# Local attention and two feed-forward layers on one core: loads under way limited to four

## The chip, the cores and the metric

The kernel runs on one core of a Trainium2 chip. A core has a matrix engine (PE, with its weight loads PEld), a vector engine (DVE), a scalar engine (ACT), a general engine (POOL) and a sync engine (SP), each with its own program, and 16 DMA engines that move data between the chip's memory and the on-chip buffers. The metric is the device time of one execution in microseconds, as the median of several runs. Before the change it is 648.09 us (three runs, 647.77 to 649.55).

## What is computed

Three stages follow one another on 1536 tokens (2 batches of 768), all in float32:

```python
# attention: 8 heads of 64, window 16, blocks of 32
k_sum = k.reshape(B, H, nb, block, D).max(axis=3)
v_sum = v.reshape(B, H, nb, block, D).mean(axis=3)
scores_l = scale * q @ k.T            # kept where |i - j| < 16
scores_s = scale * q @ k_sum.T + log(block)
a = softmax(concat(scores_l, scores_s)); x = a @ concat(v, v_sum)
# layer 1: RMS norm, gate and value (512 -> 1536), back to 512
xn = x / rms * rms_g
y = (silu(xn @ w_gate) * (xn @ w_val)) @ w_out
# layer 2: 512 -> 2048 -> 512
r = maximum(y @ w_in, 0); out = (s * r * r + b) @ w_out2
```

## The kernel before

**Attention, then the layers.** The attention works on 12 tiles of 128 tokens (two halves of 64 queries, four head pairs). For a tile PE multiplies queries with a key window and with the block maxima (line 522), DVE adds the mask and finds the extremes (541), ACT takes the exponentials (548), PE transposes the weights (559) and multiplies with the value window and the block means (578), DVE normalises (596), and after the RMS norm (611 to 619) PE transposes the tile into `x` (627). From about 70 us on the matrix products of the layers take over (`mm12`, lines 726 to 730, and 849 to 852). Each weight comes as a 512 KB tile of 64-bit words, which ACT and DVE turn into a float32 (205, 214 to 216) and which is then split into a high and a low part (227, 231).

**Loads.** Every load is a DMA that SP issues: keys `load_k` (273), queries `load_q` (440), value windows `load_v` (277), transposed values `load_vt` (290), the vector of constants (157), weights `w_load` (199). `spread_v` (312) copies the block means, 24 partitions, from one value slot to others, on the chip. SP runs its program in order: an issue that has to wait holds all issues behind it. Eight semaphores serve the loads in turn, so in the kernel before the change a load waits for the landing of the eighth load in front of it, and for whatever frees its target buffer (three query tiles, three raw weight tiles, one value buffer shared by the two batches).

**What sets the order.** The attention part is written as a list of tasks with an engine, a duration, dependencies and a rank (`plan`, from line 434 on). `give_out` plays these through a small model of the engines and so fixes the order of each engine's program. The layers' part is written out in order (`moe`).

Of the kernel before, what the change touches and what calls it, by code (L numbers as in the profile page):

```python
# [11 lines left out]
I32 = mybir.dt.int32  # L12
# [6 lines left out]
NB, NH, SEQ, HD = 2, 8, 768, 64  # L19
# [16 lines left out]
NSUB = NB * SEQ // SUB  # L36
TPS = SUB // 128
HEAD = 3
LAT = 0.09
AHEAD = 4.0  # L40
IDLE = 0.6
PTENG = ("ACT",)
QB = 3
# [11 lines left out]
def kernel(ctx: ExitStack, tc: tile.TileContext, q_t, k_t, v_w, v_t, w_gate, w_val, w_out, w_in2, w_out2, vecs, out):  # L55
    nc = tc.nc
# [19 lines left out]
    def banks(*ids):  # L76

        turn = [0]

        def take():  # L80
            i = ids[turn[0] % len(ids)]
            turn[0] += 1
            return psp.tile([128, 512], F32, tag=f"b{i}", name=f"b{i}")
        return take
# [21 lines left out]
    vec = const.tile([128, DM + 2], F32, name="vec")  # L106
    gbc, sbc, bbc = vec[:, 0:DM], vec[:, DM:DM + 1], vec[:, DM + 1:DM + 2]
    junk = const.tile([128, DM], mybir.dt.bfloat16, name="junk")
    qc = [const.tile([128, NPAIR, 2, HQ], F32, name=f"q{i}") for i in range(QB)]
# [8 lines left out]
    vt0 = xyp.tile([128, 2 * KD * SUB], F32, tag="xy", name="vt")  # L118
# [4 lines left out]
    kst = [t[:, 0:NPAIR * KL].rearrange("p (j s) -> p j s", j=NPAIR) for t in kb]  # L123
# [24 lines left out]
    def consts_mask2():  # L148
# [3 lines left out]
        for i, p0, o in ((0, 0, 0), (2, 64, HQ + WIN)):  # L152
            nc.gpsimd.tensor_copy(masks[i], m)
            nc.gpsimd.memset(masks[i][p0:p0 + 64, o:o + WIN], NEG / scale)

    def load_small():
        nc.sync.dma_start(out=vec, in_=vecs)


    later = [[] for _ in range(8)]  # L160
# [22 lines left out]
    units = []  # L183
# [12 lines left out]

    def w_load(i):
        t = rawp.tile([128, 512, 2], I32, tag="raw", name="raw")
        nc.sync.dma_start(out=t.rearrange("p f c -> p (f c)"), in_=units[i].bitcast(I32))
        raw_t[i] = t  # L200

    def w_scale(i):
# [31 lines left out]
    def w_split(i):  # L234
        w_high(i)
        w_low(i)

    steps = [w_load, w_scale, w_bits, w_split]
    used = [0]
    live = [0]  # L240
# [29 lines left out]


    def load_k(b, j):
        nc.sync.dma_start(out=kst[b][:, j], in_=k_t[b, j])

    def load_v(b, s0, n):
        t = vst[b][s0 // NTL][0:KW, s0 % NTL:s0 % NTL + n]
        nc.sync.dma_start(out=t.rearrange("p s h d -> p (s h d)"), in_=v_w[b, s0 // n])

    def ones_v(b, s0, n):
        rows = KC if s0 < (4 if b == 0 else 2) else KW  # L280
# [6 lines left out]
    vs = vt0[:, NPAIR * SEQ:NPAIR * SEQ + 512]  # L287

    def load_vt(b, j):
        nc.sync.dma_start(out=vt0[:, j * SEQ:(j + 1) * SEQ], in_=v_t[b, j])  # L290

    def sum_vt(b, j):
        c0 = j * 128 + KW
# [15 lines left out]
    def spread_v(b, s0, n):  # L309
        a = vst[b][0][KW:KC, 0:2].rearrange("p (o e) h d -> p o (e h d)", o=1).broadcast_to([NS, n // 2, 2 * NH * VH])  # L310
        o = vst[b][s0 // NTL][KW:KC, s0 % NTL:s0 % NTL + n]
        nc.sync.dma_start(out=o.rearrange("p (o e) h d -> p o (e h d)", e=2), in_=a)


    tasks = []
# [3 lines left out]
    def task(eng, us, fn, deps=(), rank=0.0, take=(), give=(), bank=None, free=(), more=0.09):  # L319

        t = dict(eng=eng, us=us, fn=fn, deps=[d for d in deps if d is not None], rank=rank, take=take, give=give,
                 bank=bank, free=free, more=more, end=None)
        tasks.append(t)
        return t
# [3 lines left out]
    def give_out():  # L328
# [22 lines left out]
        while left:  # L351
            moved = False
            for e in ("SP", "PE", "ACT", "DVE", "POOL"):
                if clock[e] > now + 1e-9:
                    continue
                for z in pending[e]:
                    t = z[2]
                    if any(d["end"] is None or d["end"] + LAT > now + 1e-9 for d in t["deps"]):
                        continue
# [25 lines left out]
                    for k, o in t["give"]:  # L385
                        ends[k][o["slot"][k]] = t["end"] + LAT
                    for o in t["free"]:
                        o["freed"] = t["end"] + LAT
                        bank_free.append((o["freed"], o["b"]))
# [13 lines left out]
            nxt += [v for k in rings for v in ends[k].values() if v > now]  # L403
            nxt += [t["end"] + LAT for t in tasks if t["end"] is not None and t["end"] + LAT > now + 1e-9]
            assert nxt, [z[2]["why"] if "why" in z[2] else (e, z[0]) for e in pending for z in pending[e][:3]]
            now = min(nxt) + 1e-6
            at = clock["PE"] + IDLE
            if now > at and any(x[0] <= at for x in bank_free) and ident_at[0]["end"] is not None and ident_at[0]["end"] + LAT < at and pending["PE"]:

# [7 lines left out]
    def dve(n):  # L417
        return 0.07 + 1.042e-3 * n

    def act(n):  # L420
        return 0.13 + 0.74e-3 * n
# [7 lines left out]
    def plan(x):  # L429
# [6 lines left out]
        def lk(b, j, rank):  # L436
            K[b, j] = task("SP", mb(128 * KL * 4), lambda: load_k(b, j), rank=rank)

        def load_q(i):
            nc.sync.dma_start(out=qc[i % QB].rearrange("p j c q -> p (j c q)"), in_=q_t[i])  # L440

        def lq(i, rank, deps=()):
            Q[i] = task("SP", mb(128 * 512 * 4), lambda: load_q(i), deps, rank=rank)

        def lvt(b, j, rank):
            VL[b, j] = task("SP", mb(128 * 768 * 4), lambda: load_vt(b, j), [SV[0, j]] if b else (), rank=rank)

        def lv(b, t, rank):
            V[b, t] = task("SP", mb(96 * 16 * VH * 4), lambda: load_v(b, 2 * t, 2), rank=rank)
            O[b, t] = task("POOL", 0.12, lambda: ones_v(b, 2 * t, 2), [V[b, t]], rank=rank)  # L450
# [10 lines left out]
        for t in range(1, NTL):  # L461
            lv(0, t, t - 1.5)
        sml = task("SP", mb(128 * 514 * 4), load_small, rank=1.2)
        for j in range(NPAIR):
            lk(1, j, 4 + j)
# [64 lines left out]
        for n, (i, g) in enumerate(us):  # L530
            b, t = divmod(i, NTL)
# [30 lines left out]
            e = PTENG[n % len(PTENG)]  # L562
# [51 lines left out]
            def do_ss(i=i):  # L614
# [5 lines left out]
                out=X_of[i], in0=X_of[i], scalar=box["ss", i][:, 1:2], in1=gbc, op0=ALU.mult, op1=ALU.mult), [S, sml], n - 1)  # L620
# [20 lines left out]
            h = task("ACT", act(512), lambda f=two_x: f(0), [ET], n - 1.2)  # L641
# [5 lines left out]
        def weight(u, rank):  # L647
            l = task("SP", mb(128 * 1024 * 4), lambda: w_load(u), rank=rank - WLEAD, take=("raw",))
            s = task("ACT", act(512), lambda: w_scale(u), [l], rank, take=("wa",))
            ops = []  # L650
            prev = s
            for k in range(3):
                def bits(k=k):
                    if k == 0:
                        ops.extend(w_ops(u))
                    ops[k]()
                prev = task("DVE", (0.45, 0.72, 0.72)[k], bits, [prev], rank + 0.1 * k, give=(("raw", l),) if k == 2 else ())
            hh = task("ACT", act(512), lambda: w_high(u), [prev], rank + 0.5, take=("wh",))
            ll = task("POOL", 1.34, lambda: w_low(u), [hh], rank + 0.5, take=("wl",), give=(("wa", s),))
            W[u] = (hh, ll)  # L660
        wr = WRANK
        for u in range(2 * HEAD + MORE):
            weight(u, wr[u] if u < len(wr) else wr[-1] + 3 * (u - len(wr) + 1))
# [5 lines left out]
        for s in range(NSUB):  # L669
            for j in range(HEAD):  # L670
                rk = FR[s] + j * FS
# [39 lines left out]
                a = task("ACT", act(512), lambda f=do_u: f(0), [got[0][2]], rr, take=("u",))  # L711
                b_ = task("DVE", dve(512), lambda f=do_u: f(1), [a], rr, free=(got[0][0],))
                c = task("DVE", dve(512), lambda f=do_v: f(0), [b_, got[1][2]], rr, free=(got[1][0],))
                d = task("ACT", act(512), lambda f=do_v: f(1), [c, *((*free_of[j], box.get("hi")) if s == 0 else ())], rr)
# [47 lines left out]
    def moe(x, ps_m):  # L762
# [24 lines left out]
        def s1(m):  # L787
            if m < HEAD:
                return
            w = next_w()  # L790
            us = [gate(m, w, s) for s in range(NSUB)]
            yield
            w = next_w()
            for s in range(NSUB):
                val(m, w, s, us[s])
            yield
# [72 lines left out]
    give_out()  # L869
    n = 2 * HEAD + MORE  # L870
    prog[:] = [n, n, n, n]
    used[0] = live[0] = 2 * HEAD
    for _ in moe(x, banks(*range(8))):
# [69 lines left out]
```

## Time and profile before

| | us |
|---|---|
| median of 3 runs | 648.09 |
| profiled execution | 647.01 |
| its span | 645.2 |
| PE busy | 622.8 |
| DVE busy | 378.1 |
| ACT busy | 259.8 |
| POOL busy | 141.7 |

The profile shows one execution. Its span runs from the first to the last instruction; some 1.8 us lie around it. A gap on an engine is put down to what ended it: another engine, a landing, or "issue", which means that the engine waited for nothing that the profile shows. The DMA tables tell how many bytes each queue moved in a stretch and what share of the 16 engines' time that took; a stretch can show more than 100%, since packets that start in it may end behind it. The chain of waits is followed back from the last instruction, at each step to what released it.

### The profile page before, as it was taken

The numbers are of one execution on the slowest core, as the hardware profiler recorded it, in microseconds if no ns is written. First come the engines' busy times: TensorE is split into PE (matmuls) and PEld (weight loads), VectorE is DVE, ScalarE is ACT, GpSimd is POOL, SyncE is SP. The second block draws the span as 40 slices with busy tenths as digits, with TensorE's granted clock in tenths as the row PEclk, the third lists the DMA queues.
The fourth block names the chain that finished last, engine by engine and source line by source line (L and its number), as shares of the span: only waits on it lengthen the run. The fifth ranks groups of instructions, "written<-read, shape, count | busy, mean of one in ns | idle before, by whom it ended". The sixth has DMA issues, their size and how long they took to land.

```text
span 645.2 us, 9632 instructions
## 1 busy us (share of the span) xinstructions
PE 622.8 (97%) x3816; PEld 514.3 (80%) x3816; DVE 378.1 (59%) x731; ACT 259.8 (40%) x524; POOL 141.7 (22%) x159
## 2 busy tenths in 40 slices
PE   5588999999999999999999999999999999999998
PEld 3576788888888888888888888888888888888886
DVE  5469886325851555544556767870388457845532
ACT  2576986334433333212333345542554045404400
POOL 2253856322311111111111111100221022103100
PEclk9889999999999999999999999999999999999999
DMA  9979622003440112221122212230212321210022
GB/s 294 230 264 257 193 60 74 1 1 98 131 130 28 42 63 66 86 61 53 62 65 69 64 65 67 65 100 31 56 46 67 94 62 42 66 61 0 2 98 99
DMA packets 17494, 55.04 MB, mean 85 GB/s; under 512 B 2000, under 2 KB 2256, under 8 KB 17448
## 3 DMA queue, kind: packets, MB, share of 16 engines
q1 hardware_dynamic: 17448, 54.42, 27.7%
q8 instruction: 30, 0.49, 0.3%
q14 instruction: 16, 0.13, 0.1%
HBM read 50.35 MB, written 3.15 MB: 83 GB/s over the span
## 4 chain that ended last, share of the span: by engine, by line
PE 91%; DVE 3%; issue 2%; DMA 1%; ACT 1%; SPq 0%; POOL 0%; POOLq 0%
PE b L726 22%; PE b L730 22%; PE b L727 22%; PE b L852 7%; PE b L850 7%; PE b L849 7%; PE b L559 2%; PE b L522 2%; PE b L578 2%; DMA vt<-in_v_t_dram 1%; PE b L627 1%; DVE vt L294 1%; DVE P L541 0%; DVE km L284 0%; ACT P L548 0%
## 5 line engine op out<-in xcount | busy, mean ns | idle before, releaser
L231 POOL TENSOR_TENSOR wl<-wa,wh 128x512 fp32r<-128x512 f32 x68 | 89.1, 1318 | 389.3 <-ACT wh L227 316.0
L726 PE MATMUL b<-x,wh 128*128 128x512 f32 x288 | 113.7, 395 | 0.1
L727 PE MATMUL b<-x,wl 128*128 128x512 f32 x288 | 112.2, 390 | 0.0
L227 ACT ACTIVATE wh<-wa 128x512 fp32r<-128x512 f32 x68 | 41.5, 627 | 97.2 <-PE b L852 45.5
L730 PE MATMUL b<-x,wh 128*128 128x512 f32 x288 | 77.8, 392 | 0.0
L850 PE MATMUL b<-wl,hg 128*128 128x512 f32 (+1 forms) x196 | 75.1, 385 | 0.0
L849 PE MATMUL b<-wh,hg 128*128 128x512 f32 (+1 forms) x196 | 75.1, 385 | 0.0
L726 PE MATMUL b<-y,wh 128*128 128x512 f32 x192 | 74.7, 389 | 0.0
L727 PE MATMUL b<-y,wl 128*128 128x512 f32 x192 | 74.7, 389 | 0.0
L831 DVE SCALAR_TENSOR_TENSOR b<-u,vec 128x512 f32<-128x512 f32 x48 | 50.7, 1057 | 35.6 <-ACT u L830 35.6
L726 PEld LDWEIGHTS b<-x,wh 128*128 128x128 f32 x288 | 54.1, 188 | 11.3 <-ACT x L638 0.4
L727 PEld LDWEIGHTS b<-x,wl 128*128 128x128 f32 x288 | 54.1, 188 | 10.7
L730 PEld LDWEIGHTS b<-x,wh 128*128 128x128 f32 x288 | 53.5, 188 | 11.0
L726 PE MATMUL b<-hg,wh 128*128 128x512 f32 x144 | 56.0, 389 | 0.0
L727 PE MATMUL b<-hg,wl 128*128 128x512 f32 x144 | 56.0, 389 | 0.0
L751 DVE SCALAR_TENSOR_TENSOR hg<-b,vec,hg 128x512 fp32r<-128x512 f32 x48 | 36.0, 749 | 28.1 <-ACT hg L750 28.1
L852 PE MATMUL b<-wh,hg 128*128 128x512 f32 (+1 forms) x196 | 51.5, 385 | 0.0
L730 PE MATMUL b<-y,wh 128*128 128x512 f32 x192 | 51.3, 389 | 0.0
L216 DVE SCALAR_TENSOR_TENSOR wa<-raw,wa 128x512 int32<-128x512 int32 x68 | 50.0, 735 | 2.0
L750 ACT ACTIVATE hg<-b,vec 128x512 fp32r<-128x512 f32 x48 | 33.0, 687 | 43.0 <-DVE b L831 43.0
L858 DVE TENSOR_TENSOR part<-b,part 128x512 f32<-128x512 f32 (+1 forms) x37 | 24.4, 673 | 43.5 <-PE b L852 43.5
L215 DVE SCALAR_TENSOR_TENSOR wa<-raw,wa 128x512 int32<-128x512 int32 x68 | 47.0, 691 | 2.0
(85 smaller groups left out, 947.2 us busy)
## 6 DMA issues: line engine op xcount, KB each, us to landing
raw<-in_w_out_dram SPq DMA_DIRECT2D x28, 512.0 KB, 3.5
raw<-in_w_in_dram SPq DMA_DIRECT2D x16, 512.0 KB, 4.1
raw<-in_w_gate_dram SPq DMA_DIRECT2D x12, 512.0 KB, 3.6
raw<-in_w_val_dram SPq DMA_DIRECT2D x12, 512.0 KB, 3.6
hg<-in_k_t_dram SPq DMA_DIRECT2D x8, 400.0 KB, 10.0
q<-in_q_t_dram SPq DMA_DIRECT2D x12, 256.0 KB, 7.1
vt<-in_v_t_dram SPq DMA_DIRECT2D x8, 384.0 KB, 8.3
out_dram<-part SPq DMA_DIRECT2D x11, 256.0 KB, 2.0
```

What stands on the lines that cost most here:

```text
L215: lambda: nc.vector.scalar_tensor_tensor(out=ai, in0=hi, scalar=-0x80000000, in1=ai, op0=ALU.bitwise_and, op1=ALU.bitwise_or),
L216: lambda: nc.vector.scalar_tensor_tensor(out=ai, in0=lo, scalar=29, in1=ai, op0=ALU.logical_shift_right, op1=ALU.bitwise_or),
L227: nc.scalar.activation(out=r(h), in_=a_t[i], func=AF.Copy)
L231: nc.gpsimd.tensor_tensor(out=r(lo), in0=a_t.pop(i), in1=high[i], op=ALU.subtract)
L726: nc.tensor.matmul(ps, r(hi[:, kk * 128:(kk + 1) * 128]), xh, start=kk == 0, stop=False)
L727: nc.tensor.matmul(ps, r(lo[:, kk * 128:(kk + 1) * 128]), xh, start=False, stop=False)
L730: nc.tensor.matmul(ps, r(hi[:, kk * 128:(kk + 1) * 128]), r(act(kk, 1)), start=False, stop=kk == 3)
L751: nc.vector.scalar_tensor_tensor(out=r(dst[1]), in0=ps, scalar=bias, in1=dst[0], op0=ALU.add, op1=ALU.subtract)
L831: after(0, lambda u=u, ps=ps: nc.vector.scalar_tensor_tensor(out=ps, in0=u, scalar=sbc[:, 0:1], in1=u, op0=ALU.mult, op1=ALU.mult))
L849: nc.tensor.matmul(acc, gh, r(ws[e][0][:, cs]), start=e == 0, stop=False)
L850: nc.tensor.matmul(acc, gh, r(ws[e][1][:, cs]), start=False, stop=False)
L852: nc.tensor.matmul(acc, r(ge[e][:, 1]), r(ws[e][0][:, cs]), start=False, stop=e == 3)
```

## The change

Seven kinds of load, all but the store of the result, are now issued through one function. It keeps the list of what it has sent, and from the fifth load on it adds a dependency on the landing of the load four places in front.

```diff
+OUT = 4
...
+    sent = []
+
+    def fetch(out, in_):
+
+        d = nc.sync.dma_start(out=out, in_=in_).ins
+        if len(sent) >= OUT:
+            tc.add_manual_dep(d, sent[-OUT].name, mybir.DependencyInfo(mybir.DependencyClass.Sync, mybir.DependencyReason.DATA),
+                              reason="transfers under way")
+        sent.append(d)
+
     def load_small():
-        nc.sync.dma_start(out=vec, in_=vecs)
+        fetch(out=vec, in_=vecs)
...
-        nc.sync.dma_start(out=t.rearrange("p f c -> p (f c)"), in_=units[i].bitcast(I32))
+        fetch(out=t.rearrange("p f c -> p (f c)"), in_=units[i].bitcast(I32))
```

The other five calls (`load_k`, `load_v`, `load_vt`, `spread_v`, `load_q`) change in the same way. The programs of PE, DVE, ACT and POOL are the same instruction for instruction, and SP issues the same transfers in the same order. What differs is the semaphore that a load names: DMAHW0 to DMAHW7 are given out in turn, load by load.

On SP at the start of the program, before the change, the first waits stand at the ninth load:

```order
L273 DMA hg<-in_k_t_dram 128x800
L440 DMA q_99<-in_q_t_dram 128x512
L273 DMA hg<-in_k_t_dram 128x800 x3
L290 DMA vt<-in_v_t_dram 128x768 x3
L277 DMA hg<-in_v_w_dram 96x1056 [waits DMAHW0_49]
L290 DMA vt<-in_v_t_dram 128x768 [waits DMAHW1_49]
L440 DMA q_100<-in_q_t_dram 128x512 [waits DMAHW2_49]
```

The same place after the change:

```order
L161 DMA hg<-in_k_t_dram 128x800
L161 DMA q_99<-in_q_t_dram 128x512
L161 DMA hg<-in_k_t_dram 128x800 x2
L161 DMA hg<-in_k_t_dram 128x800 [waits DMAHW0_49]
L161 DMA vt<-in_v_t_dram 128x768 [waits DMAHW1_49]
L161 DMA vt<-in_v_t_dram 128x768 [waits DMAHW2_49]
L161 DMA vt<-in_v_t_dram 128x768 [waits DMAHW3_49]
L161 DMA hg<-in_v_w_dram 96x1056 [waits DMAHW4_49]
```

The fifth load (the fourth key load) now names the first one's landing, and the first value window, the ninth, names that of the fifth where it named that of the first.

On SP at the first spread, before the change (the spread also waits for ACT and POOL, which write what it copies):

```order
L277 DMA hg<-in_v_w_dram 96x1056 [waits DMAHW1_49]
L312 DMA hg<-hg 24x1056 [waits DMAHW2_49,Activation_49,Pool_49]
L312 DMA hg<-hg 24x3x1056 [waits DMAHW3_49]
L440 DMA q_100<-in_q_t_dram 128x512 [waits DMAHW4_49,PE_49]
L199 DMA raw<-in_w_gate_dram 128x1024 [waits DMAHW5_49]
```

And after it:

```order
L161 DMA hg<-in_v_w_dram 96x1056 [waits DMAHW5_49]
L161 DMA hg<-hg 24x1056 [waits DMAHW6_49,Activation_49,Pool_49]
L161 DMA hg<-hg 24x3x1056 [waits DMAHW7_49]
L161 DMA q_100<-in_q_t_dram 128x512 [waits DMAHW0_49,PE_49]
L161 DMA raw<-in_w_gate_dram 128x1024 [waits DMAHW1_49]
```

Nothing changes places; each row names a landing four loads nearer.

## Rows read from the trace of the kernel before

**Rows 1.** The profile's page: span, busy time, the queue of instruction packets.

```profile
span 645.2 us, 9632 instructions
PE 622.8 (97%) x3816; PEld 514.3 (80%) x3816; DVE 378.1 (59%) x731; ACT 259.8 (40%) x524; POOL 141.7 (22%) x159
...
q8 instruction: 30, 0.49, 0.3%
```

**Rows 2.** Stages: us, busy PE PEld DVE ACT POOL, granted clock, DMA share, GB/s.

```profile
5.00:10.00 5.00, 3.23 (x64) 2.26 (x64) 3.09 (x4) 0.00 (x0) 0.00 (x0) 1.00 1.02 385
...
20.00:25.00 5.00, 2.75 (x66) 2.51 (x59) 2.38 (x22) 2.66 (x10) 1.96 (x4) 0.83 1.07 237
25.00:30.00 5.00, 3.26 (x91) 2.76 (x90) 2.88 (x20) 3.54 (x11) 1.99 (x4) 0.83 1.03 200
30.00:35.00 5.00, 2.15 (x16) 2.03 (x16) 0.36 (x3) 0.63 (x2) 1.01 (x1) 0.51 1.02 296
...
50.00:55.00 5.00, 3.91 (x24) 2.93 (x23) 5.00 (x10) 2.04 (x5) 1.02 (x1) 1.00 1.06 298
...
100.00:640.00 540.00, 540.00 (x2435) 446.93 (x2434) 303.10 (x451) 191.90 (x338) 95.50 (x79) 1.00 0.20 62
```

**Rows 3.** Chain of waits, 18 to 46 us: start, length, what.

```profile
20.60 2.25 issue
...
28.26 4.58 issue
32.85 0.71 PE b L578 x9
33.56 1.04 PE b L559 x4
...
40.70 0.84 issue
...
44.25 1.54 POOL sm L590
...
45.81 0.42 DVE xn L596
```

**Rows 4.** Issue to landing of the loads issued at 0.7, 10.7 and 22.4 us.

```profile
L273 SPq DMA_DIRECT2D hg<-in_k_t_dram x1: 383/383/383, 0.7 to 0.7; - x1
DMA to landing us min/median/max: 3.0/3.0/3.0
...
L440 SPq DMA_DIRECT2D q<-in_q_t_dram x1: 346/346/346, 10.7 to 10.7; - x1
DMA to landing us min/median/max: 10.0/10.0/10.0
...
L277 SPq DMA_DIRECT2D hg<-in_v_w_dram x1: 429/429/429, 22.4 to 22.4; - x1
DMA to landing us min/median/max: 11.7/11.7/11.7
```

**Rows 5.** Instruction packets that start in 20.2:20.4, 30.0:30.2, 39.0:39.2, 72.8:73.0 us.

```profile
q8 instruction: 1, 0.02, 39.5%
...
q8 instruction: 1, 0.02, 41.7%
...
q8 instruction: 1, 0.02, 32.5%
...
q8 instruction: 1, 0.02, 30.6%
```

**Rows 6.** POOL in order of time, 39 to 45 us.

```profile
39.41 0.13 POOL L281 MEMSET hg<- 96x32 f32 x1
...
43.42 0.19 POOL L616 TENSOR_SCALAR ss<-ss 128x1 f32<-128x1 f32 x1 [2.29 <-ACT junk L611]
```

**Rows 7.** Chain of waits, 70 to 73 us.

```profile
71.64 0.58 PE b L559 x4
```

More of the change, by code (lines that the diff above doesn't have):

```diff
@@ L272, in load_k @@
     def load_k(b, j):
-        nc.sync.dma_start(out=kst[b][:, j], in_=k_t[b, j])
+        fetch(out=kst[b][:, j], in_=k_t[b, j])
     def load_v(b, s0, n):
         t = vst[b][s0 // NTL][0:KW, s0 % NTL:s0 % NTL + n]
-        nc.sync.dma_start(out=t.rearrange("p s h d -> p (s h d)"), in_=v_w[b, s0 // n])
+        fetch(out=t.rearrange("p s h d -> p (s h d)"), in_=v_w[b, s0 // n])
     def ones_v(b, s0, n):
@@ L289, in load_vt @@
     def load_vt(b, j):
-        nc.sync.dma_start(out=vt0[:, j * SEQ:(j + 1) * SEQ], in_=v_t[b, j])
+        fetch(out=vt0[:, j * SEQ:(j + 1) * SEQ], in_=v_t[b, j])
     def sum_vt(b, j):
@@ L311, in spread_v @@
         o = vst[b][s0 // NTL][KW:KC, s0 % NTL:s0 % NTL + n]
-        nc.sync.dma_start(out=o.rearrange("p (o e) h d -> p o (e h d)", e=2), in_=a)
+        fetch(out=o.rearrange("p (o e) h d -> p o (e h d)", e=2), in_=a)
     tasks = []
@@ L439, in load_q @@
         def load_q(i):
-            nc.sync.dma_start(out=qc[i % QB].rearrange("p j c q -> p (j c q)"), in_=q_t[i])
+            fetch(out=qc[i % QB].rearrange("p j c q -> p (j c q)"), in_=q_t[i])
         def lq(i, rank, deps=()):
```

## The prediction

> **What bounds the kernel now.** I read the page first. The span is 645.2 us and TensorE (PE) is busy for 622.8 of it [rows 1]: the kernel is bound by PE, and what can be won is the 22 us in which PE does nothing. The table by stages tells where they lie: from 100 to 640 us PE is busy for 540.00 of 540 us, with the clock granted in full, so no load and no wait matters there. The idle time is in the attention part, in front of 70 us: 2.75 of 5 us busy from 20 to 25, 3.26 from 25 to 30, 2.15 from 30 to 35, where the granted clock is 0.83, 0.83 and 0.51 [rows 2]. In the same stretches the DMA column stands at 1.02 to 1.07: the 16 DMA engines always have work there. The change touches loads alone, so these 35 us decide.
>
> Next the chain of waits through that stretch [rows 3]. It runs on PE and it holds three gaps that are put down to "issue", time in which the engine waited for nothing that the profile shows: 2.25 us at 20.60, 4.58 at 28.26, 0.84 at 40.70, in sum 7.67. All three stand in the middle of a run of like matmuls, and no load is named as what ended them. Behind the third the chain goes over ACT and POOL to DVE at 45.81, and DVE is busy for 5.00 of 5 us from 50 to 55 [rows 2]. So time lost on PE in the gaps is handed on to the end.
>
> What ends these gaps? The queues' table has a second kind of packet: 30 of kind "instruction" on queue 8, 0.49 MB in all, 16 KB each [rows 1]. PE's page has 3816 matmuls and 3816 weight loads; 7632 over 30 is 254 instructions a packet, 64 bytes each. These packets are PE's program. Asked by short windows, the DMA table shows one of them at 20.2 to 20.4 us, one at 30.0 to 30.2 and one at 39.0 to 39.2 [rows 5]. Each stands inside a gap or just ahead of it, and PE goes on 2.5 to 2.9 us behind the window's start: at 22.85, 32.85 and 41.54, each gap's start and length added. I read the gaps as PE having run out of program, with the next block late.
>
> Why late? PE got the block in front at 22.85 and the next packet starts at 30.0: if it is asked for when the block in front comes into use, it stood for about 7.2 us. From 32.85 to 39.0 it is 6.2 us. That is the size of the loads' own wait: with nothing in front a 400 KB load lands 3.0 us after its issue; but the load issued at 10.7 us takes 10.0 and that of 22.4 takes 11.7 [rows 4]. These stand behind up to seven others. The instruction packets seem to stand in that line too. When a block is asked for, no row says; this is the weak step.
>
> **The change part by part.** On PE, DVE, ACT and POOL not one instruction moves; on SP the order is the same too. What changes is the wait of each load: for the landing of the fourth one in front, where it was the eighth. The dependency adds no instruction.
>
> The added wait itself. Does the queue run dry with three loads ahead? The load of 0.7 us needed 3.0 us from issue to landing with an empty queue. At the 385 GB/s of 5 to 10 us a 400 KB load takes 1.06 us, so 1.9 us of the 3.0 are turnaround. Three such loads in front are worth 3.2 us; two query loads of 256 KB (0.68 each) and one of 396 (1.05) are worth 2.4. Both are over 1.9, and at the 200 to 237 GB/s of 20 to 30 us three loads cover over 5 us. So the engines stay fed, loads land when they did, and I cost the wait at 0. SP is in order: behind a load that waits stand the next loads only, and the spreads of L312; what waits for them is priced below. If the cover is gone, rival D has the price. Behind 100 us the raw ring of three tiles already holds fewer than four loads under way: 0.
>
> The gaps. With four in place of eight under way, the line that a packet of program joins is about half as long: 3.6 to 5.0 us where it was 7.2 to 10.0 [rows 3 to 5].
> - Gap 1: the packet comes about 5 us earlier, half of the 10.0 us that the load of 10.7 took; 2.25 us would do. All 2.25 goes.
> - Gap 2: without gap 1 PE begins that block at 20.6. The packet starts 3.6 to 5.0 later, and 2.7 us behind its start PE can go on (30.1 to 32.85): 26.9 to 28.3. PE gets there at 28.26 - 2.25 = 26.0. What is left is 0.9 to 2.3 of 4.58; I take 1.6, a gain of 3.0.
> - Gap 3: from 32.85 to 40.70 PE needs 7.85 us for the block; the packet needs 3.1 (half of 6.2) and 2.5. It is in time: 0.84 goes.
> The sum is 2.25 + 3.0 + 0.84 = 6.1 us. From below it is bounded by nothing gained, 0; from above by all 7.67 and what the clock gives back: the transposes of L559 at 33.56 take 1.04 us for four, and 0.58 at 71.64 [rows 3, 7], and L578 and two more transposes stand beside them, so up to 0.9 more.
>
> What is late next? The landings don't come earlier, the DMA engines being full. The first user to feel it is POOL's memset at 39.41 on the value window issued at 22.4, landed 11.7 later at 34.1 [rows 4, 6]: 5.3 us of slack. A shift of 6.1 asks 0.8 more; POOL feeds the chain at 45.81, but has idle time of its own, so I take 0.5 off. That leaves 5.6 us. Against the profiled execution's own 647.01 us (the span and 1.8 around it) that is 641.4; the median of the three runs is 1.08 higher, 648.09, and gives 642.5.
>
> A rule of the Trainium skill speaks against this, in "DMA: Bandwidth & Descriptors", section "Queues, rings and completion order": each DMA engine takes turns between the queues with work, a packet at a time, so a block on its own queue would wait for one packet, not for a line of loads. By it the sum would be 0 (rival C). The trace is on the other side so far: 6.2 to 7.2 us between one block's use and the next packet, where 3 us is a whole empty load. Another, "Runtime: NRT & Kernel Launch", section "Instruction fetch mechanics", says that the sequencer fetches its next 16 KiB block while it runs the current one and that crossing a boundary is mostly hidden. The block's size agrees (0.49 MB over 30); hidden it is from 100 to 640 us, and not in the 4.58 us at 28.26.
>
> **The rivals.**
> A, the forecast: the gaps shrink or go, and DVE and POOL follow: 4 to 8.5 us, 639.6 to 644.1. For it: the packets at the gaps, and waits like the loads' own.
> B, the gaps go but the loads are the next bound: landings are tied to a full DMA queue, and users other than the memset have slack that I have not all read; or the line shortens by less than half. 2 to 4 us are left: 644.1 to 646.1. For it: DMA at 1.0 until 35 us. Against it: the 5.3 us.
> C, the packet's wait does not hang on how many loads stand in line, but on the piece that the engine has in hand: no change, 647.5 to 648.7. For it: the page's rule, and packets are slow just where the rate is 200 GB/s, so the gaps could come from slow pieces. Against it: the packet at 72.8 to 73.0 [rows 5], which lies in faster traffic; it is no proof.
> D, four are too few, slower: the 16 engines don't finish together, so the round trip under traffic may be longer than the 3.0 us of an empty queue. Four loads of 1.06 cover 4.24 us; from there on each lands later. Pool's slack of 5.3 us on a landing at 34.1 is used up when loads come 16% slower, at a round trip of 4.9 us. At 5.3 us, a quarter slower, the window lands 8.5 us late, 3.2 more than the slack, and with the gaps kept the time is 651.3. For it: nothing but that the overlap is thin (2.4 against 1.9) at the query loads. Against it: the slow stretch from 20 us on covers more than it needs.
> That the waits are not there is excluded by the order: each load from the fifth on names a landing.
>
> **How the numbers follow.** A 0.47, B 0.20, C 0.19, D 0.14. A measurement of this kernel can tell about 0.3%, 1.9 us. A and nearly all of B are faster: 0.66. C and the edges of B and D are the same: 0.19. Slower 0.15. The likeliest is A at 642.5, with its own range 639.6 to 644.1. The range for 8 in 10 goes from 640.0, which leaves out the last of A, over B and C to 649.0, and leaves D out.
>
> **What would show it.** In the chain of the changed kernel the "issue" gap at 20.60 is gone and that of 28.26 is under 2.5 us; PE is busier, and its granted clock higher, from 20 to 35 us; instruction packets come earlier against PE's work; a load takes 4 to 6 us from issue to landing where it took 10 to 11.7; the DMA rate from 5 to 35 us is unchanged; DVE's full stretch begins some 5 us before 45.81. I am wrong if both gaps stay at their size while loads land in half the time (C), if PE's idle time moves to waits that name a load (B), or if the rate from 5 to 15 us falls (D).

## The result and the profile after

The changed kernel takes 642.33 us in the median of 20 runs (639.53 to 649.0), the kernel before 648.24 in the median of 20 (646.84 to 651.36). The ratio is 0.9914, with a 95% interval of 0.9898 to 0.9931: 5.6 us faster by the ratio, 4.5 to 6.6, and 5.9 by the two medians. The forecast was 642.5.

The profiled execution of the changed kernel is the longest of its 20, 649.0 us, so I read it beside a second one, "again", that took 644.09. Both lie above the median. Line numbers behind 156 are 11 higher than before the change, and all loads now have line 161.

The spans, first of that profile, then of "again":

```profile
span 647.2 us, 9628 instructions
```

```profile
span 642.3 us, 9628 instructions
```

PE's idle time in the changed kernel, 0 to 80 us, by releaser (who waits, for whom: us in all, times, the longest; "issue" is what the prediction calls gaps):

```profile
PE b L589 <- ACT PT L580: 7.5, 4, 4.2
PE b L533 <- DMA q<-in_q_t_dram: 5.6, 2, 4.7
...
PE b L589 <- issue: 0.2, 1, 0.2
```

The same view of "again":

```profile
PE b L638 <- issue: 2.7, 1, 2.7
```

The gaps of 2.25 and 4.58 us [rows 3] are gone from both. PE runs through their places: at 21.42, where it now stands in the work that the first gap held up, its matmuls follow one another without a stop, and the 32 matmuls that the second gap had cut in two (23 and 9) stand in one piece.

```profile
21.33 0.26 PE L533 MATMUL b<-km,q 64*64 64x24 f32 x8
21.42 0.38 PE L533 MATMUL b<-hg,q 64*64 64x96 f32 x8
...
25.32 1.15 PE L589 MATMUL b<-hg,PT 120*64 120x66 f32 x32
```

The third gap (0.84 before) is gone from the first profile and is 2.7 us in the second. The instruction packet that ended the second gap at 30.0 to 30.2 before [rows 5] now starts at 22.7 to 22.9, before PE gets to that place at 26.0:

```profile
q8 instruction: 1, 0.02, 40.2%
```

The stages of the changed kernel, with the columns of [rows 2]:

```profile
5.00:10.00 5.00, 2.21 (x52) 1.51 (x48) 2.32 (x3) 0.00 (x0) 0.00 (x0) 1.00 0.97 328
...
20.00:25.00 5.00, 5.00 (x155) 3.93 (x155) 4.76 (x35) 4.18 (x15) 2.11 (x3) 1.00 1.01 247
25.00:30.00 5.00, 3.99 (x88) 3.13 (x77) 2.77 (x17) 4.66 (x18) 2.73 (x6) 1.00 0.77 146
30.00:35.00 5.00, 4.21 (x109) 3.64 (x110) 3.43 (x18) 4.62 (x14) 1.95 (x4) 1.00 1.01 334
...
60.00:65.00 5.00, 2.27 (x24) 1.45 (x18) 3.89 (x19) 1.74 (x5) 4.61 (x5) 1.00 0.91 182
65.00:70.00 5.00, 2.98 (x42) 2.52 (x46) 2.51 (x15) 4.18 (x13) 2.14 (x4) 0.57 0.75 164
70.00:80.00 10.00, 10.00 (x114) 8.60 (x108) 5.35 (x25) 6.38 (x19) 2.95 (x5) 0.70 0.71 230
```

From 20 to 35 us PE is busy for 13.2 of 15 us where it was 8.16, and the granted clock is 1.00 throughout (0.83, 0.83, 0.51 before). The other side stands in the first row: 328 GB/s where eight loads gave 385, and the DMA share is 0.97 where it was 1.02. (In the second profiles of the two kernels the rates are 326 and 361.)

The chain of waits shows where the gain is given back (start, length, what):

```profile
28.50 6.54 DMA hg<-in_v_w_dram
...
35.09 0.12 POOL hg L292
35.21 0.99 POOL sm L601
...
36.23 0.43 DVE xn L607
...
56.44 9.30 DMA raw<-in_w_gate_dram
...
65.82 0.10 ACT wa L216
...
66.39 0.59 ACT PT L580
...
67.02 1.15 PE b L589 x16
```

The chain no longer runs on PE here. Until 35.0 us it is on a value window, which was issued at 28.50, landed 6.54 later at 35.04 and was waited for by POOL's memset. That is the window and the memset of [rows 4, 6]; it landed at 34.1 before. The second profile has the same wait:

```profile
35.22 0.12 POOL L292 MEMSET hg<- 96x32 f32 x1 [3.03 <-DMA hg<-in_v_w_dram]
```

Behind it this long execution has one more wait: a weight tile that took 9.30 us held ACT, which works in order, and ACT held PE for 4.18 us.

```profile
62.18 0.66 PE L638 MATMUL b<-ident,xn 128*128 128x128 f32 x4 [0.51 <-DVE xn L630]
67.02 1.15 PE L589 MATMUL b<-part,PT 120*64 120x66 f32 x16 [4.18 <-ACT PT L580]
```

The transposes at 62.18 started at 67.95 in the kernel before, so up to this point the changed kernel was 5.8 us ahead. The wait took 3.8 of that (4.18 where it was 0.40), and PE came back at a granted clock of 0.57 and then 0.70, where it was 1.00 before. From the products at 67.02 to the end of the span it took 580.2 us, against 576.2 from the same products at 69.00 in the kernel before: 4.0 us more. So this execution ends 2.0 us behind. In the second profile the same products start without that wait, at 66.10, and have the same 576.2 us behind them; 645.2 - 642.3 is the 2.9 us by which they come earlier.

The same products in the kernel before, then in "again":

```profile
69.00 0.69 PE b L578 x16
```

```profile
66.10 0.69 PE b L589 x16
```

### The profile page after: what moved, and what is told of

It is laid out like the page before. It is cut to its first block, busy times and chain, and to the rows that moved or that the text cites. A ratio compares the mean times of both kernels' runs of the same rounds, so it can differ in the third digit from the quotient of the medians.

```text
span 647.2 us, 9628 instructions
## 1 busy us (share of the span) xinstructions
PE 625.7 (97%) x3816; PEld 516.3 (80%) x3816; DVE 377.8 (58%) x731; ACT 260.3 (40%) x524; POOL 141.3 (22%) x159
## 4 chain that ended last, share of the span: by engine, by line
PE 89%; DMA 8%; DVE 1%; issue 0%; ACT 0%; POOL 0%; SPq 0%; ACTq 0%
PE b L737 22%; PE b L738 22%; PE b L741 22%; PE b L863 7%; PE b L860 7%; PE b L861 7%; DMA hg<-in_v_w_dram 3%; DMA vt<-in_v_t_dram 3%; DMA raw<-in_w_gate_dram 1%; DMA q<-in_q_t_dram 1%; PE b L589 1%; PE b L570 1%; PE b L533 1%; PE b L638 0%; PE b L425 0%
## 5 line engine op out<-in xcount | busy, mean ns | idle before, releaser
L738 PEld LDWEIGHTS b<-x,wl 128*128 128x128 f32 x288 | 54.6, 189 | 10.7
L227 DVE SCALAR_TENSOR_TENSOR wa<-raw,wa 128x512 int32<-128x512 int32 x68 | 50.0, 735 | 2.0
L216 ACT ACTIVATE wa<-raw 128x512 f32<-128x512 f32 x68 | 44.4, 659 | 11.3 <-POOL wl L242 7.6
```

Source lines behind the costliest of these rows:

```text
L216: nc.scalar.activation(out=a, in_=raw_t[i][:, :, 1].bitcast(F32), func=AF.Copy, scale=2.0 ** -112)
L227: lambda: nc.vector.scalar_tensor_tensor(out=ai, in0=lo, scalar=29, in1=ai, op0=ALU.logical_shift_right, op1=ALU.bitwise_or),
L738: nc.tensor.matmul(ps, r(lo[:, kk * 128:(kk + 1) * 128]), xh, start=False, stop=False)
```

## The experiments

Theory: PE's program comes in blocks of 256 instructions; with eight loads under way the next block comes late, and PE stands at a block's end. Rivals: the gaps belong to a piece of work, or the change wins by something else, such as the order in which loads land.

**again**: the changed kernel for a second profile, no edit. 

> The changed kernel once more, for a second profile, since the first profiled execution took 649.0 us and the median is 642.3. Theory (program blocks stand in line with loads; with four loads under way the line is short): no issue gap over 0.5 us at the two block ends near 20 and 28 us, PE idle from 15 to 35 us under 4 us where it was 7; time 640 to 645. Rival (the loads become the bound, the line only half as long): gaps gone but new waits that name loads, and the span within 2 us of the kernel before. Rival (gaps not tied to the line): gaps of 2.2 and 4.6 us again.


644.09 us, read above: the first two gaps are gone and the third is 2.7. At the two block ends the theory is borne out. The rival of the loads as the next bound is borne out in part: the chain now runs over loads, while the span is 2.9 us below that of the kernel before, more than the 2 us that the rival allowed. Against "before2", the next run, it is 0.2 us.

**before2**: the kernel before for a second profile, no edit. 

> The kernel before once more, for a second profile. Theory: gaps with no named releaser in front of PE instructions 449 and 705 again, of 1.5 to 4 and 2.5 to 6 us; time 646 to 650. Rival (the gaps of the first profile were an accident): none or at other counts.


644.24 us in its one execution, less than expected, and less than all 20 runs of the same kernel above. The gaps are there again, in front of the same matmuls at PE records 450 and 705 (a record is a matmul or a weight load; counts here are good to one or two), 1.47 and 3.76 us long, so their length changes from one execution to the next:

```profile
22.28 0.31 PE L522 MATMUL b<-hg,q 64*64 64x96 f32 x3 [1.47 <-issue]
...
29.91 0.46 PE L578 MATMUL b<-hg,PT 120*64 120x66 f32 x9 [3.76 <-issue]
```

**shift2**: eight loads under way; the first tile's products are made twice at 10 us. 

> The kernel before (eight under way); the 32 small products of the first query tile (line 522) are made twice, the second time with the same values, about 1 us of PE at 10 us where it then waits for ACT: 64 more PE instructions and nothing else. Theory (PE runs out of program at each 256th instruction): the gaps keep their counts 449, 705 and 961 and so stand 64 instructions nearer the front of the work: gap 1 of 1.5 to 4 us at the start of the third tile's products of line 522, gap 2 of 2 to 6 us inside the fourth tile's products of line 522 instead of line 578. Rival (a hidden wait that belongs to that piece of work): the gaps stay at the same matmuls, now number 513 and 769. Time 646 to 650 by both.

```diff
-                for j in range(NPAIR):
+                for j in (*range(NPAIR), *(range(NPAIR) if i == 0 else ())):
                     for o, n in ((0, KW), (KW, NS)):
```

The expectations count the doubled products as 64 more PE instructions, here and in the runs below. The page shows twice that: the 32 doubled calls are 64 matmuls (3880 where there were 3816), each with its weight load, so 128 records. The places in the work that the expectations name for the gaps are off by as much.

644.17 us, ratio 0.9935 (0.9918 to 0.9952): more work and nothing taken away, and 4.2 us faster. The expected time was 646 to 650, so no theory had foretold this. The third gap stands at its count, 962 of PE's records, and so in another piece of work: in the products of line 522, where it was in the transposes of line 627.

```profile
30.71 0.24 PE L522 MATMUL b<-km,q 64*64 64x24 f32 x2
33.68 0.25 PE L522 MATMUL b<-km,q 64*64 64x24 f32 x3 [2.73 <-issue]
```

The first two gaps, which the theory expected at their counts, are gone: nothing stands at record 450, and 0.18 us at 705. The packet that came at 20.2 to 20.4 before [rows 5] starts at 14.2 to 14.4 here:

```profile
q8 instruction: 1, 0.02, 35.2%
```

With 128 more records in front, the end of the block before it (record 194) is reached at 10.7 us and no longer at 17.1. In the kernel before, that record lies behind a stretch of 4.63 us in which PE only transposes a constant (line 414) while it waits for ACT, here it lies in front of it. I read this as the block having been late not for the loads' sake alone, but also because it was asked for late; no row shows the asking. That the gaps are a hidden wait of one piece of work is refuted by the third.

**shift**: a first form of it, 32 small products on constants. 

> The kernel before (eight loads under way) with 32 small matmuls on constants (64 PE instructions with their weight loads) added where PE waits at 11 us; their results are not used. Theory (PE runs out of program at the end of a block of 256 instructions): the gaps stay at the same count of PE instructions from the start (449 and 705), so they move 64 instructions to the front in the work: gap 1 to the start of the third tile's products of line 527, gap 2 into the fourth tile's products of line 527 in place of line 583. Lengths 2 to 5 us, time 646 to 650. Rival (a hidden wait of that piece of work, such as a bank or a buffer): the gaps stay in front of the same matmul, which is now number 513 and 769 of the program.

```diff
+                    for k in range(32):
+                        nc.tensor.matmul(ps[0:64, 0:24], ident[0:64, 0:64], ident[0:64, 0:24], start=True, stop=True)
```

It missed its aim: the products took 7.0 us of PE and so moved more than the block's end. The time was still no longer, 646.94 us, ratio 0.9985 (0.9965 to 1.0005). In its profile the first two gaps are gone, and 0.8 us stands at record 962, here in the products of line 527 (522 without the edit).

**shift_tile4**: the control, with the fifth tile's products doubled (`i == 4`). 

> Control for the doubled products: the kernel before (eight loads) with the products of the fifth query tile doubled in place of the first, so the 64 more PE instructions stand behind the first two gaps. Theory (what counts is where a block ends, not that PE does more): gaps 1 and 2 stay at counts 449 and 705 in front of the same matmuls as before, 1.5 to 4 and 2 to 5 us, and the time stays at 646.5 to 649.5. Rival (a busier PE or its clock is what helps): faster by 3 to 5 us, 643 to 645.


651.89 us, ratio 1.0058 (1.0035 to 1.0081): slower by more than expected. Both gaps stay in front of their matmuls, 2.68 and 6.11 us, and further gaps of 1.31 and 2.4 us stand at records 962 and 1985. The profiled execution is the longest of the ten (655.55), so its gaps may be longer than those of a typical run.

```profile
25.03 0.31 PE L522 MATMUL b<-hg,q 64*64 64x96 f32 x3 [2.68 <-issue]
35.01 0.71 PE L578 MATMUL b<-hg,PT 120*64 120x66 f32 x9 [6.11 <-issue]
43.42 0.25 PE L522 MATMUL b<-km,q 64*64 64x24 f32 x3 [1.31 <-issue]
```

So it is not the busier PE that helps: the same extra work at another place does not. What differs between the two kernels is where in the work the blocks end.

**four_shift**: the change and the doubled first products together. 

> The change (four loads under way) and the doubled first products (64 more PE instructions at 10 us) together. Theory (both win by the same thing, the program block in time): the gains don't add; the doubling alone gave 4.2 us and the limit alone 5.9, together 641 to 645. Rival (the limit wins by something else, such as the order in which loads land): the gains add to about 10 us, 637 to 639.


642.39 us, ratio 0.991 (0.9886 to 0.9935). The gains of 5.9 and 4.2 us don't add, as the theory said: what one takes away is not there for the other. No gap is over 0.2 us, and what is left names ACT and loads.

```profile
PE b L533 <- DMA q<-in_q_t_dram: 5.5, 3, 4.6
PE b L589 <- ACT PT L580: 4.4, 4, 1.7
...
PE b L589 <- issue: 0.2, 1, 0.2
```

**out6, out3, out2**: other limits, one number changed each.

```diff
-OUT = 4
+OUT = 6
```

Six: 

> Six loads under way. Theory: the line of loads is three quarters of that of eight, so the wait of a program block lies between: gap 1 (2.25 us with eight) 0 to 1, gap 2 (4.6) 1.5 to 3.5; the time between the two kernels, 643 to 646. Rival (the queue must not run dry, and only depth counts): like eight at 648, or better than four by the loads that come earlier, 640 to 642. Rival (gaps not tied to the line): gaps as with eight, 648.


645.13 us, ratio 0.9966 (0.9947 to 0.9986). The time is as expected, the gaps are not: 3.62 and 2.39 us. The loads of 17.4 and 18.5 us still take 10.5 and 11.0 us from issue to landing, so the line was no shorter in time.

```profile
DMA to landing us min/median/max: 10.5/10.5/10.5
...
DMA to landing us min/median/max: 11.0/11.0/11.0
```

Three: 

> Three loads under way. Theory: no gaps at block ends, but two loads in front (2.1 us at full rate) cover the turnaround of 1.9 only just, and less than it at the query loads: between four (642) and two (666), 645 to 653. Rival (only the gaps count): 641 to 643.


646.47 us, ratio 0.9974 (0.9954 to 0.9994). The time is inside the expected range, but the expected absence of gaps is not borne out: 0.5 us stands at record 450 and 2.6 at 705. The profiled execution is the longest of its ten (649.42).

Two: 

> Two loads under way in place of four. Theory: gaps stay away (the line is shorter still), but one load in front (about 1.06 us) does not cover the turnaround of 1.9 us, so the engines run dry: the rate from 5 to 15 us falls from about 300 to about 200 GB/s, loads land a third later, slower than four by 8 to 20 us: 650 to 662. Rival (the time hangs on the gaps alone): like four, 641 to 644. Rival (gaps not tied to the line): gaps return.


666.4 us, ratio 1.0288 (1.0255 to 1.0321). There is no gap at all, and the kernel is 18 us slower than the one with eight, more than expected. From 10 to 15 us the DMA engines are busy for 0.66 of the time.

```profile
10.00:15.00 5.00, 3.84 (x27) 2.69 (x28) 2.76 (x3) 0.00 (x0) 0.00 (x0) 1.00 0.66 213
```

**early**: four for loads 5 to 18, eight behind. 

> The limit of four only for loads 5 to 18, those in front of the first spread (issued up to 15 us in the kernel before); from the spread on a load waits for the eighth again. Theory: the blocks that end gaps 1 and 2 are asked for while the line is short, so both gaps go or nearly (the second under 2.5 us), the third (0.8 us) may come back or grow, loads behind 20 us are issued earlier: 641 to 645, most of the change's gain. Rival (the gain comes from later loads that land in a better order): 647 to 649.

```diff
-        if len(sent) >= OUT:
+        if OUT <= len(sent) < 18:
```

644.08 us, ratio 0.9931 (0.992 to 0.9943). The time fits and the mechanism doesn't: the profile has gaps of 1.77 and 3.02 us, about those of before2, which took as long (644.24).

```profile
21.42 0.31 PE L533 MATMUL b<-hg,q 64*64 64x96 f32 x3 [1.77 <-issue]
...
28.31 0.71 PE L589 MATMUL b<-hg,PT 120*64 120x66 f32 x9 [3.02 <-issue]
```

This profile does not show what makes the median faster.

**late**: four from load 19 on (`if len(sent) >= 18`). 

> The limit of four only from the first spread on (load 19 and later); the first 18 loads stand eight deep as before. Theory: gap 1 as before (2 us), gap 2 shorter but not gone, since the eight early loads still stand in line at 20 us; gain 0 to 3 us: 645 to 648.5. Rival (the gain comes from the later loads): 641 to 644.


643.36 us, ratio 0.9924 (0.9909 to 0.9939). A miss: it is faster than expected. The first gap stays, as expected (3.64 us), but the second is gone. A likely reason, which no row shows, is that the second block's packet meets the late loads, four deep, and no longer the early ones: it starts 4.9 us behind the landing of the packet in front of it (22.0 to 26.9), where that was 8.6 and 6.5 us in the two profiles of the kernel before.

```profile
PE b L533 <- issue: 3.6, 1, 3.6
PE b L638 <- issue: 0.7, 1, 0.7
PE b L589 <- issue: 0.2, 1, 0.2
```

**late_shift**: both edits. 

> The limit of four only from the first spread on, and the doubled first products. Theory: the doubling takes gaps 1 and 2 without making the first 18 loads wait, the limit keeps the third gap (2.9 us in the doubled kernel) under 1.5 us: the best of these kernels, 639.5 to 642.5. Rival (the loads that land are the bound once the gaps are gone): no better than each alone, 642.5 to 645.


642.37 us, ratio 0.992 (0.9901 to 0.9939). The gaps are down to 1.2 us in sum, and the time is no better than the change's. So the rival is borne out in its time: once the gaps are gone, something else is the bound. Which engine or load that is, one profile does not settle.

For the kernels with PE's program as it was, this table takes PE's "issue" time of the first 80 us off the span. Each row is one profiled execution, all in us.

| kernel | span | issue | rest |
|---|---|---|---|
| before | 645.2 | 7.9 | 637.3 |
| before2 | 642.5 | 6.1 | 636.4 |
| six | 644.9 | 8.3 | 636.6 |
| early | 642.3 | 5.8 | 636.5 |
| late | 640.5 | 4.5 | 636.0 |
| four (again) | 642.3 | 2.7 | 639.6 |
| four (the long execution) | 647.2 | 0.2 | 647.0 |
| three | 647.6 | 3.4 | 644.2 |
| two | 663.4 | 0 | 663.4 |

Down to "late" the rest is the same within 1.3 us: there the span is the gaps' time and a constant. In "again", with four throughout, the rest is 2.3 to 3.6 us more, with three some 7 to 8 and with two 26 to 27. I read that as the price of fewer loads. It is rough: the profile with three is of its longest execution, 3 us above the median, and the long one with four holds the wait for the weight tile and the lower clock.

Every gap over 0.4 us in the fourteen profiles, 26 in all, stands at PE record 450, 705, 962, 1473 or 1985: multiples of 256 apart within one, whatever piece of work lies there.

## Why the prediction was right, step by step

- **What bounds it.** Right: the gaps were PE out of program. The count holds (450, 705, 962 in the kernels with gaps), the work at that place doesn't matter, and one doubled loop takes the first two away.
- **Gap 1**, all 2.25 us: right, in both profiles. **Gap 2**, 3.0 of 4.58 with 0.9 to 2.3 left: the gain was put too small, all of the gap went. **Gap 3**, 0.84: it is gone once and 2.7 us once.
- **The added wait at 0**: wrong in size. From 5 to 10 us the rate fell from 385 to 328 GB/s, and the value window of [rows 4] landed 1.0 us later. The limit costs some 2 us in the two profiles against the first of the kernel before, and some 3 by the table. The cover of three loads was worked out for 16 engines that move as one; what opened the holes is not shown.
- **What is late next**, POOL's memset on the window that landed at 34.1: the right place, and too cheap at 0.5 us. The memset came 4.3 us earlier (39.41 to 35.09), where PE's record 705 came 6.8 earlier (32.85 to 26.0), so about 2.5 us were given back there.
- **The weight tile** that holds ACT at 65.7 us was not in the prediction. With the lower clock behind it, it makes the run of 649.0 us. Why it took 9.30 us to land is not shown.
- **The sum of 5.6** holds by two errors that nearly cancel, which is luck in part. Up to 62 us of the first profile the gaps gave 7.7 us where the prediction had 6.1, the loads took 1.9 back where it had 0.5, and 5.8 us were won. In "again" the gaps gave 5.2, since the third one grew, the loads took 2.3, and 2.9 us were won. So neither whole profile shows the 5.6 to 5.9 us of the medians; the first one does up to its last wait.
- **The rivals.** C's forecast of no change is refuted. D (too few loads) is what happens at two, and in part at four. B is half true: the loads are the next bound, but they leave more of the gain than its 2 to 4 us.
- **The line.** That a block's packet waits in one line with the loads is not settled. For it: six loads still take over 10 us to land and still have gaps, four take 5.4 to 6.5 and mostly have none. Against it: with four, "again" has a packet at 33.4 to 33.6, 7.2 us behind the end of the block before it, and with three there is a gap of 2.6 us. No row tells when a block is asked for, but the steady part hints at it. There, from 130 us on, each packet starts when PE is some 41 records (27 to 42 in the kernel before) ahead of the end of the block that lies two in front of it; that is earlier than the prediction took it. If it is asked for at that place in the loaded part too, the three packets of the three gaps started late by this much (us from PE's records 154, 410 and 666 to the packet's start):

| loads under way | first | second | third |
|---|---|---|---|
| eight (before, before2) | 7.4, 7.1 | 10.2, 7.2 | 11.6, 10.3 |
| six | 8.3 | 9.4 | 8.7 |
| late: eight, then four | 7.7 | 7.6 | 5.5 |
| early: four, then eight | 6.0 | 6.2 | 10.5 |
| three | 5.4 | 5.2 | 8.2 |
| four (first profile, again) | 4.0, 3.8 | 1.7, 1.7 | 5.9, 7.9 |
| two | 5.2 | 2.1 | 1.5 |

Fewer loads under way mostly go with an earlier packet, and "early" and "late" change places from the first to the third. It is not in proportion to their number, the second and third figures also hold PE's own stops and the packet in front, and "shift2" has 4.2 us for its first packet with eight loads under way. By the rule of the Trainium skill that the prediction cites ("DMA: Bandwidth & Descriptors", section "Queues, rings and completion order"), that each DMA engine takes turns between the queues packet by packet, the depth would not matter. It does matter here, to the gaps as to this table, so that rule alone does not tell the time.

## What to carry to other kernels

An idle stretch of an engine that waits for nothing, in the middle of a run of like instructions, is worth counting. Here it came at the same count of instructions in every execution, and meant that the engine was out of program; both fewer loads under way and more instructions in front of the block's end took it away. A limit on loads had two sides here: with eight or six the packets of program came late, with two the DMA engines were left without work (0.66 busy from 10 to 15 us). Before pricing such a limit, read the slack of the users of each load, not of the nearest one alone.

## What the runs showed that I had not expected

More PE work can be faster: 32 doubled products made the kernel 0.65% faster in one place (ratio 0.9918 to 0.9952) and 0.58% slower in another (1.0035 to 1.0081). And the same kernel's gaps differ from one execution to the next: 2.25 and 4.58 us in one, 1.47 and 3.76 in the other, with 2.7 us between the spans.
